# Four layers on one core: causal tiles of 64 queries shared by two heads, and the gates of a segment in one run

## The chip, the core and the metric

The kernel runs on one core of a Trainium2 chip as one program. Its time is the device time of one execution in microseconds. The engines are named as the profile names them: PE (TensorE, matrix products, with PEld for its weight loads), DVE (VectorE), ACT (ScalarE), POOL (GpSimd) and SP (SyncE, which here issues nearly all DMAs).

## The reference, cut to what matters

Two kinds of layer alternate over x of 2048 tokens x 512: an attention with a compressed memory (32 heads of 16, four segments of 512 tokens), and a gated feed-forward network with 1792 hidden columns. The weights of both attention layers are the same, and so are those of both networks.

```python
def _A_ref(x, wq, wk, wv, wo, beta):          # H = 32, Dh = 16, N = 4 segments, L = 512
    ...
    phi = lambda t: jnp.where(t > 0, t + 1.0, jnp.exp(t))
    mask = (ar[:, None] < ar[None, :]) * -1e9
    g = sigmoid(beta)
    for s in range(N):
        logits = einsum('bhqd,bhkd->bhqk', qs, ks) * scale + mask
        a_dot = einsum('bhqk,bhkd->bhqd', softmax(logits), vs)
        pq = phi(qs)
        num = einsum('bhld,bhde->bhle', pq, M)
        den = einsum('bhld,bhd->bhl', pq, z)[..., None] + 1e-06
        outs.append(g * (num / den) + (1.0 - g) * a_dot)
        pk = phi(ks)
        M = M + einsum('bhld,bhle->bhde', pk, vs)
        z = z + einsum('bhld->bhd', pk)
    return concat(outs) @ wo

def _B_ref(x, w_gate, w_up, w_down):
    return gelu(x @ w_gate) * (x @ w_up) @ w_down

x = x + _A_ref(_layernorm(x), ...)
x = x + _B_ref(_layernorm(x), ...)
x = x + _A_ref(_layernorm(x), ...)
x = x + _B_ref(_layernorm(x), ...)
```

## The kernel before

The work is cut into eight segment steps k = 0 to 7: four segments of the first pair of layers, then four of the second. x stays in SBUF (`x_sb`). Step k has an object `Att(k)` and an object `Ffn(k)`; segment k + 4 starts from the x that `Ffn(k)` left.

**Who sets the order.** The order on every engine is written out in full when the program is built. A planner (`Clocks`, `Engine`, `Item`) keeps an estimated clock for each engine; at each step of PE it picks the next thing that is ready by those clocks: a pair of score rounds (`score`), a memory product (`mem_event`), or an `Item`, a product of several matmuls that needs one of eight PSUM banks. Each item has a due time, and jobs of the other engines have slacks, all from the table `POLICY`. Where nothing is ready, PE gets a product of a constant (`warm`) as a filler. On the chip, nothing is reordered: each engine works through its list and waits by semaphores.

**Attention.** `qk` and `v` items make q, k (transposed: 4 blocks b of 128 rows, each 8 heads of 16 rows) and v. A "round" of scores is 256 columns on each of four row tiles of PE (32 rows each): it covers four of the eight heads of a block, the even ones (`par` 0, from `kf`, 16 rows) or the odd ones (`par` 1, from `kB`, a copy of k in which the even heads' rows are zero). A head has five rounds (`PIECES`), made of keys in tiles of 128 and the queries from there on: 512 + 384 + 256 + 128 = 1280 columns. So a block has 2 x 5 rounds, and `score` issues two rounds at a time (L848). One exp for 128 x 1024 empties each of the two pairs of PSUM banks into `pt` (ACT, L1285), and POOL zeroes what lies above the diagonal (L1291). After a head group's five rounds a "flush" (`flush_item`, L864) multiplies `pt` with v, on four column tiles of PE, into one bank; v carries a column that gives the softmax's sum. DVE transposes the result (L879), divides, transposes back (L894) and adds the memory's part (L897); `wo` follows.

`kB` is made by DVE (L591) for k < 4 and by four DMAs on SP per block for k of 4 and more (L588).

**Memory.** phi is exp on ACT (L648), a minimum on POOL (L666) and an addition on DVE (L652), which also sums phi k over the tokens (`zk`, by the accumulator). phi k is transposed by DMA, and the update (L769) multiplies it with v; `macc` and `zacc` hold M and z.

**Feed-forward.** The norm's rows (`Norm`, L447 to L477) are transposed by DMA, or for the steps in `BY_PE` on PE (L507 to L509). Of the 14 gate tiles of a step, 9 are copied out of PSUM by DVE or ACT (L408, L409) and get their Gelu in SBUF (L1046); the last 5 (`direct`) get it from PSUM (L972). In step 7 all 14 do (L959). DVE multiplies each up tile into the gate (L994), and `down` follows, added to x by DVE (L934).

**Dense products** go through `product`: whole (L421), or as four matmuls of 32 output rows side by side (L418), whichever avoids a change of tiling on PE.

Of the kernel before, what the change touches and what calls it, by code (L numbers as in the profile page):

```python
# [11 lines left out]
ACT = mybir.ActivationFunctionType  # L12
# [30 lines left out]
NO_DIAG = 1  # L43


def narrow(pieces, par):

    if par:
        return pieces
    return [(ki, q0 + o, min(n, 64) if n == P else n, c0 + o) for ki, q0, n, c0 in pieces  # L50
            for o in ((0, P // 2) if n == P else (0,))]
# [5 lines left out]
SETS = 3  # L57

URGENT, SOON, NORMAL = -4.0, -1.5, 0.0
XN_BUFS = 4  # L60
# [4 lines left out]
POLICY = dict(  # L65
    flush_wait=152.105, piece_slack=40.738, kb_slack=10.905, mem_slack=-2.348, margin=2.56, qk_due=0.594,
    e_q=-0.77, e_k=1.073, exp_slack=-18.49, e_slack=11.096, phi_slack=6.459, gelu_slack=-0.034, act_evict=5.372,
    first_evict=-0.382, gate_step=0.0, up_due=1.256, up_step=0.012, down_due=3.948, down_step=1.013,
    upd_due=-0.62, v0_due=1.254, x1_at=0.158, x2_at=5.744, x3_at=0.964, x3_load=17.129, cut_slack=-0.231,
    direct=5, gelu_tiles=1, phi_pool=0, kb_dve=4, rounds=2, early=0.939, starve=0.658, ahead=0.286, near=-3.652,  # L70
    cap=7, soon=1.448, am_slack=1.081, mem_wait=0.156)
# [11 lines left out]
class Engine:  # L83
# [4 lines left out]
    def __init__(self, overlap=0.0):  # L88
        self.free, self.overlap, self.jobs, self.table = 0.0, overlap, [], "exp"
        self.only, self.rival, self.port = None, None, 0.0  # L90

    def post(self, ready, slack, *steps, table=None, taken=None):

        self.jobs.append((ready, slack, steps, table, taken if taken is not None else []))

# [12 lines left out]
    def serve(self, now):  # L108

        self.jobs = [j for j in self.jobs if not j[4]]  # L110
        jobs = [j for j in self.jobs if not self.only or j[3] in (None, self.only)]
        if not jobs:
            return False
        start = max(self.free, min(j[0] for j in jobs) + self.LATENCY)
# [5 lines left out]
        self.jobs.remove(job)  # L120
        t = ready
# [18 lines left out]
class Clocks:  # L140
# [6 lines left out]
    def __init__(self):  # L147
# [7 lines left out]
        self.ev = {}  # L155

# [19 lines left out]
    def serve(self):  # L176

        again = True
        while again:
# [9 lines left out]
            first = min(self.engines, key=lambda e: max(e.free, min((j[0] for j in e.jobs), default=1e9)))  # L189
            again |= first.serve(self.pe) or any(e.serve(self.pe) for e in self.engines)  # L190
# [52 lines left out]

class Box:
# [9 lines left out]
class Policy:  # L254
    def __init__(self, values):
        self.__dict__.update(values)


def order(pol, nc, cst, seg, wrk, psp, A_x, A_wq, A_wk, A_wv, A_wo, A_beta, B_x, B_w_gate, B_w_up, B_w_down, out):
# [70 lines left out]
    bd = cst.tile([P, P], F32, name="bd")  # L330
    nc.gpsimd.memset(bd[:], 1.0)
    nc.gpsimd.affine_select(out=bd[:], in_=bd[:], pattern=[[-16, 8], [0, 16]], compare_op=ALU.is_ge,
                            fill=0.0, base=0, channel_multiplier=1)
    nc.gpsimd.affine_select(out=bd[:], in_=bd[:], pattern=[[16, 8], [0, 16]], compare_op=ALU.is_ge,
                            fill=0.0, base=15, channel_multiplier=-1)
    kBs = [cst.tile([P, KT, L], BF16, name=f"kB{i}") for i in range(SETS)]
    for kB in kBs[1:]:
        nc.vector.memset(kB[:], 0.0)
    mask2 = cst.tile([P, 2 * DH], F32, name="mask2")
    nc.vector.reduce_sum(out=mask2[:], in_=bd[:].rearrange("p (c n) -> p n c", c=4), axis=mybir.AxisListType.X)  # L340
    maskB = mask2[:, DH:DH + 1]

    tmp_e = cst.tile([P, H], F32, name="tmp_e")
    tmp_e2 = cst.tile([P, H], F32, name="tmp_e2")
    cden = cst.tile([P, H], BF16, name="cden")
    macc = cst.tile([P, 4, 2 * DH], F32, name="macc")
    e2x = cst.tile([P, 2, 2, 2, 4 * TPS], F32, name="e2x")
    zacc = cst.tile([P, 4], F32, name="zacc")
    vaugs = [cst.tile([P, TPS, VW + 15], BF16, name=f"vaug{i}")[:] for i in range(SETS)]
    vaugs.append(gel_sb[:].rearrange("p f l -> p (f l)")[:, 0:TPS * (VW + 15)].rearrange("p (t v) -> p t v", t=TPS))  # L350

    def by_head(va):
        return va[:, :, 0:VW].rearrange("p t (h e) -> p t h e", e=DH + 1)
# [1062 lines left out]
```

## Time and profile before

| | |
|---|---|
| time, median of 3 runs | 547.69 us (547.14 to 548.39) |
| the profiled execution's own time | 547.77 us |
| its span | 546.1 us |
| granted TensorE clock | 1.00 |
| PE busy | 535.6 us, 98% |
| DVE busy | 442.4 us, 81% |
| ACT busy | 445.5 us, 82% |
| POOL busy | 278.8 us, 51% |
| HBM read, written | 9.71 MB, 2.10 MB |

The busy time of an engine is a sum over stages with different limits. In the groups of instructions a row has line, engine, operation, output <- inputs, shapes and count, then the busy time in us and the mean of one in ns, then the idle time before it and what ended it. Matmuls overlap, so the mean duration of one is longer than its share of PE's time.

### The profile page before, as it was taken

The page shows a single profiled execution, that of the slowest core. Times are in us where ns is not written, and L with a number is a line of the kernel's source. Part 1 is how long each engine was busy: PE and PEld are TensorE (multiplying, and loading weights), DVE is VectorE, ACT ScalarE, POOL GpSimd, SP SyncE. Part 2 cuts the span into 40 slices and gives each one's busy share as a digit, 9 for nine tenths or more (in the row PEclk, how much of TensorE's full clock was granted, in tenths as well). Part 3 has the DMA queues.
Part 4 walks back from the last instruction along what each step waited for, and adds up shares of the span by engine and source line. Part 5 has one row for each costly group of instructions (what it writes and reads, how often), then busy time and mean ns, then how long its engine had stood idle before and what let it go on. Part 6 is the DMA issues. An engine that isn't in the chain of part 4 may idle for free.

```text
span 546.1 us, 23526 instructions
## 1 busy us (share of the span) xinstructions
PE 535.6 (98%) x10291; PEld 266.0 (49%) x10321; DVE 442.4 (81%) x880; ACT 445.5 (82%) x572; POOL 278.8 (51%) x410
## 2 busy tenths in 40 slices
PE   9999999999999999999999999999999999999997
PEld 4444444445544444444444444455454446445444
DVE  7999999779998999588987987979768796786072
ACT  5899989999999959989999899988998789910500
POOL 2687774367928847156862668724574155300000
PEclk9999999999999999999999999999999999999999
DMA  8248702500150135000224040132201003000001
GB/s 265 46 81 174 178 2 41 166 13 4 30 80 14 42 51 79 12 10 16 42 31 79 13 51 13 31 61 34 53 29 41 18 19 68 4 2 21 21 0 38
DMA packets 66983, 26.96 MB, mean 49 GB/s; under 512 B 55360, under 2 KB 66880, under 8 KB 66880
## 3 DMA queue, kind: packets, MB, share of 16 engines
q1 hardware_dynamic: 66448, 25.19, 22.9%
q8 instruction: 80, 1.31, 1.1%
q10 hardware_dynamic: 432, 0.27, 0.2%
q14 instruction: 23, 0.19, 0.1%
HBM read 9.71 MB, written 2.10 MB: 22 GB/s over the span
## 4 chain that ended last, share of the span: by engine, by line
PE 83%; DVE 12%; issue 2%; DMA 2%; ACT 0%; DVEq 0%
PE ps L418 45%; PE ps L421 21%; PE ps L848 8%; PE ps L864 6%; DVE st L447 1%; DMA phik<-e 1%; DVE byq L879 1%; PE ps L320 1%; DVE x_sb L934 1%; DVE xn L477 1%; DVE ab L887 1%; DMA xnT<-xn 1%; DVE e L652 1%; PE ps L700 1%; DVE gel_sb L408 1%
## 5 line engine op out<-in xcount | busy, mean ns | idle before, releaser
L1285 ACT ACTIVATE pt<-ps 128x1024 bf16<-128x1024 f32 x320 | 308.0, 1026 | 31.4 <-PE ps L848 22.0
L1291 POOL TENSOR_SCALAR_AFFINE_SELECT pt<-pt 128x512 bf16<-128x512 bf16 (+1 forms) x320 | 184.2, 582 | 178.0 <-ACT pt L1285 176.5
L994 DVE TENSOR_TENSOR gel_sb<-gel_sb,ps 128x512 bf16<-128x512 bf16 x112 | 75.4, 685 | 39.4 <-PE ps L421 22.2
L418 PE MATMUL ps<-wd_sb,gel_sb 128*32 128x512 bf16 (+1 forms) x1452 | 81.5, 364 | 0.0
L666 POOL TENSOR_SCALAR e<-e 128x512 bf16<-128x512 bf16 x48 | 73.8, 1541 | 5.1 <-ACT e L648 3.3
L418 PE MATMUL ps<-xnT,wg_sb 128*32 128x512 bf16 x1040 | 63.3, 380 | 0.2 <-DVE gel_sb L408 0.2
L879 DVE STREAM_TRANSPOSE byq<-ps 128x512 f32<-128x512 f32 x64 | 45.4, 709 | 17.4 <-PE ps L864 15.0
L934 DVE TENSOR_TENSOR x_sb<-x_sb,ps 128x512 bf16<-128x512 bf16 (+1 forms) x68 | 43.0, 643 | 16.5 <-PE ps L421 13.4
L418 PE MATMUL ps<-xnT,wu_sb 128*32 128x512 bf16 x956 | 55.3, 380 | 0.0
L418 PEld LDWEIGHTS <-gel_sb 128*32 128x32 bf16 x1452 | 35.9, 96 | 31.3 <-issue 6.5
L421 PE MATMUL ps<-xnT,wu_sb 128*128 128x512 bf16 x202 | 45.9, 379 | 0.7 <-issue 0.3
L421 PE MATMUL ps<-xnT,wg_sb 128*128 128x512 bf16 x178 | 40.9, 379 | 1.0 <-issue 0.5
L864 PE MATMUL ps<-pt,vaug 128*32 128x256 bf16 (+2 forms) x1568 | 40.9, 243 | 0.0
L447 DVE BATCH_NORM_STATS2 st<-x_sb 128x6 f32<-128x512 bf16 x60 | 40.5, 675 | 0.4
L418 PEld LDWEIGHTS <-wg_sb 128*32 128x32 bf16 x1040 | 26.1, 96 | 24.7 <-issue 4.2
L864 PEld LDWEIGHTS <-vaug 128*32 128x32 bf16 x1568 | 32.2, 97 | 10.0 <-issue 1.6
L418 PEld LDWEIGHTS <-wu_sb 128*32 128x32 bf16 x956 | 24.3, 97 | 25.1 <-issue 2.6
L1046 ACT ACTIVATE gel_sb<-gel_sb 128x512 bf16<-128x512 bf16 x63 | 35.0, 632 | 0.0
L418 PE MATMUL ps<-wo_sb,aT 128*32 128x512 bf16 x500 | 31.3, 380 | 0.2 <-DVE x_sb L934 0.2
L421 PEld LDWEIGHTS <-wu_sb 128*128 128x128 bf16 x209 | 19.9, 98 | 23.6 <-issue 0.2
L477 DVE TENSOR_SCALAR xn<-x_sb,mv,rs 128x512 bf16<-128x512 bf16 x64 | 30.2, 526 | 1.2 <-POOL rs L465 0.9
L848 PE MATMUL ps<-q,kf 16*128 16x256 bf16 (+1 forms) x896 | 31.0, 232 | 0.1
(128 smaller groups left out, 718.5 us busy)
## 6 DMA issues: line engine op xcount, KB each, us to landing
wg_sb<-in_B_w_gate_dram SPq DMA_DIRECT2D x8, 224.0 KB, 4.2
wu_sb<-in_B_w_up_dram SPq DMA_DIRECT2D x8, 224.0 KB, 4.1
wd_sb<-in_B_w_down_dram SPq DMA_DIRECT2D x7, 256.0 KB, 4.3
x_sb<-in_A_x_dram SPq DMA_DIRECT2D x3, 512.0 KB, 7.9
out_dram<-x_sb SPq DMA_DIRECT2D x12, 128.0 KB, 1.7
kB<-kf SPq DMA_DIRECT2D x64, 16.0 KB, 1.8
xnT<-xn SPq DMA_TRANSPOSE x48, 2.5
wv_sb<-in_A_wv_dram SPq DMA_DIRECT2D x1, 512.0 KB, 6.9
```

The costliest lines, as they stand in the source:

```text
L418: nc.tensor.matmul(out[r], lhsT=lhsT[:, r], rhs=rhs, start=start, stop=stop, tile_position=(0, 32 * c))
L421: nc.tensor.matmul(out, lhsT=lhsT, rhs=rhs, start=start, stop=stop)
L447: nc.vector.bn_stats(out=self.st6[:, 0, :], in_=x_sb[:, self.tt0 + j, :])
L477: nc.vector.tensor_scalar(out=xn[:], in0=x_sb[:, self.tt0 + j, :], scalar1=self.mv[:, j, 0:1], scalar2=self.rs[:, j, :], op0=ALU.subtract, ...
L666: return lambda: eng.tensor_scalar(out=e[0][:], in0=e[0][:], scalar1=1.0, scalar2=None, op0=ALU.min)
L848: nc.tensor.matmul(ps_all[:, pair[unit // 2], o:o + n], lhsT=lhsT[rows, b, P * ki:P * ki + P], rhs=self.q[rows, b, q0:q0 + n], start=True, ...
L864: nc.tensor.matmul(ps()[32 * j:32 * j + 32, q0:q0 + n], lhsT=self.vaug[:, ki, h * (DH + 1):h * (DH + 1) + 32], rhs=pt_all[:, slot, unit, c ...
L879: nc.vector.transpose(out=self.byq[:, par, :, :].rearrange("p a c -> p (a c)"), in_=ps()[:])
L934: ck.dve.post(ck.made(), slack, (0.15 + 0.00104 * (c1 - c0), lambda: nc.vector.tensor_tensor(out=xt, in0=xt, in1=ps()[:, 0:c1 - c0], op=AL ...
L994: ck.dve.post(ck.made(), NORMAL, (0.683, lambda: nc.vector.tensor_tensor(out=g, in0=g, in1=ps()[:], op=ALU.mult), lambda t: (ps.read(t), e ...
L1285: nc.scalar.activation(out=pt_all[:, s0, :, :].rearrange("p (h u) c -> p h (u c)", h=2), in_=ps_all[:, p0[0]:p0[1] + 1, :], func=ACT.Exp, ...
L1291: nc.gpsimd.affine_select(out=half, in_=half, pattern=[[0, w], [1, P]], compare_op=ALU.is_ge, fill=0.0, base=0, channel_multiplier=-1)
```

## The change

- **Tiles of 64 queries.** The scores of a head off the diagonal are cut at 64 queries instead of 128, and fill four rounds (`PIECES`). What is left, 64 queries against their own 64 keys at the start of each key tile, goes into one round which both heads of a pair share (`SHARED`, round `MAIN`): a 128-key product whose first 64 rows are the even head's and whose last 64 the odd head's keys. Its keys are `kX`: 64 columns in which the odd heads' rows are zero, and 128 in which the even heads' are. A block now has 9 rounds.
- `kX` is made by DVE for k = 0, and by eight DMAs on SP per block for every other k. There is one `kX` per block, so a copy waits for the scores of the step before on that block.
- The flush takes four rounds with v and the shared one with `vS`, v rearranged so that rows 0 to 63 hold the even and 64 to 127 the odd head's; two DMAs per step make it, and a flush waits for them. A flush has 40 matmuls instead of 24 or 32.
- The masks work on 64 columns, and on the shared round on 64 partitions by 256 columns, twice.
- **Gates in one run.** `direct` is 14: when the first gate of a step has been issued, the other 13 follow, no scores are issued meanwhile, and every Gelu reads PSUM.
- **The sum of phi k** comes from the update: v's extra column makes it a product of 34 columns; `zk` and `zacc` go, and one mask (`mask34`) serves M and z.
- **Start.** The constants of gate and v move from DVE to POOL, ahead of the first norm's rows; the norm of step 1 is transposed on PE; fillers are 128 columns wide instead of 512, and 32 instead of 256 ahead of a transposed tile.
- **New order.** `POLICY` has other values throughout, among them `x3_load` (the last quarter of x loads at 31.6 instead of 17.1 us of the planner's clock) and `kb_dve`.

```diff
-ROUNDS = 5
-STEPS = 8 * ROUNDS
-PIECES = [[(0, 0, 256, 0)], [(0, 256, 256, 0)], [(1, 128, 256, 0)], [(3, 384, 128, 0), (1, 384, 128, 128)],
-          [(2, 256, 256, 0)]]
+Q = P // 2
+MAIN = 4
+ROUNDS = 2 * MAIN + 1
+STEPS = KT * ROUNDS
+PIECES = [[(0, 64, 256, 0)], [(0, 320, 192, 64), (3, 448, 64, 0)], [(1, 192, 256, 0)],
+          [(2, 320, 192, 0), (1, 448, 64, 192)]]
+SHARED = [(ki, P * ki, Q, Q * ki) for ki in range(KT)]
...
-    first_evict=-0.382, gate_step=0.0, up_due=1.256, up_step=0.012, down_due=3.948, down_step=1.013,
-    upd_due=-0.62, v0_due=1.254, x1_at=0.158, x2_at=5.744, x3_at=0.964, x3_load=17.129, cut_slack=-0.231,
-    direct=5, gelu_tiles=1, phi_pool=0, kb_dve=4, rounds=2, early=0.939, starve=0.658, ahead=0.286, near=-3.652,
+POLICY = {..., 'gate_step': 0.764, 'up_due': 0.735, 'up_step': -0.024, 'down_due': 3.352, 'x3_load': 31.598, 'direct': 14, 'kb_dve': 1, 'early': 2.22, 'starve': 1.318, 'burst_slack': -4.609, 'hold': 0.287, 'late': 0.8, 'turn1': 4, 'vs_slack': 3.116}
...
+                def odd():
+                    nc.vector.tensor_scalar(out=kX[:, :, Q:], in0=keys(), scalar1=maskB, scalar2=None, op0=ALU.mult)
...
+                def copy(j, par):
+                    r = slice(32 * j + DH * par, 32 * j + DH * (par + 1))
+                    return lambda: nc.sync.dma_start(out=kX[r, :, Q:] if par else kX[r, :, 0:Q],
+                                                     in_=keys()[r] if par else keys()[r, :, 0:Q])
...
+                    for n in range(8):
+                        ck.sp.post(t, slack, (0.62, copy(n % 4, n // 4), sent if n == 7 else None))
...
-                    for j in range(4) if k >= pol.kb_dve else ():
-                        r = slice(32 * j + DH, 32 * j + 2 * DH)
-                        ck.sp.post(t, pol.kb_slack if k else URGENT, (0.62, lambda r=r: nc.sync.dma_start(
-                            out=self.kB[r, b, :], in_=self.kf[r, b, :]), kb_sent if j == 3 else None))
...
+                    ck.when(lambda: k == 0 or ("sc", k - 1, b) in ev, lambda: masked(max(t, ck.pe) if k else t))
...
+                ck.sp.post(t, pol.vs_slack, (0.62, copy(0), None), (0.62, copy(1), landed))
...
-                                                   accum_out=self.zk[:, b:b + 1] if which == "k" else None)
+                    nc.vector.scalar_tensor_tensor(out=dst, in0=src, scalar=0.0, in1=e[0][:], op0=ALU.max, op1=ALU.add)
...
-                                     rhs=by_head(self.vaug)[:, j, 8 * b + 2 * g:8 * b + 2 * g + 2, 0:DH], start=(c == 0),
+                                     rhs=by_head(self.vaug)[:, j, :, 4 * b + g, :], start=(c == 0),
...
+            for ki, q0, n, c0 in SHARED if par is None else PIECES[i % (MAIN + 1)]:
                 for j in range(4):
...
+                work = [(r + (MAIN + 1) * par, self.vaug, piece) for r in range(MAIN) for piece in PIECES[r]]
+                work += [(MAIN, self.vS, piece) for piece in SHARED]
+                for n_mm, (i, values, (ki, q0, n, c0)) in enumerate(work):
+                    for j in range(4):
...
-                              and ck.has(*[("v", k, j) for j in range(TPS)])
+                              and ck.has(("vS", k))
...
+                    if pol.direct >= FT:
+                        if self.n_gate == 1:
+                            ck.burst = FT
+                            for it in items:
+                                if it.kind == "gate" and it.after == ("xnTf", k):
+                                    it.due = -0.8
+                        ck.burst -= 1
+                        ck.act.post(ck.made(), pol.burst_slack, (0.602, lambda: nc.scalar.activation(
+                            out=gel_sb[:, ft, :], in_=ps()[:], func=ACT.Gelu_apprx_tanh),
+                            lambda t: (ps.read(t), ev.update({("gel", k, ft): t}))), table="gelu")
+                        return
...
-        if not streams or not rounds_ready(2):
+        if not streams or not rounds_ready(2) or ck.burst > pol.hold:
             return 0
...
-                nc.gpsimd.affine_select(out=half, in_=half, pattern=[[0, w], [1, P]], compare_op=ALU.is_ge, fill=0.0,
-                                        base=0, channel_multiplier=-1)
+                half = pt_all[:, slot, at[0]:4:2 if len(at) == 2 else 1, 0:Q]
+                nc.gpsimd.affine_select(out=half, in_=half, pattern=[[0, len(at)], [1, Q]], compare_op=ALU.is_ge, fill=0.0,
+                                        base=Q, channel_multiplier=-1)
+
+            def mask_shared(slot, at, par):
+                part = pt_all[Q * par:Q * (par + 1), slot, at[0]:4:2 if len(at) == 2 else 1, :]
...
-                product(ps(), warm[:], wide)
-                ck.on_pe(Clocks.MM[512])
+                product(ps()[:, 0:P], warm[:], warm[:])
+                ck.on_pe(Clocks.MM[128])
```

More of the change, by code (lines that the diff above doesn't have):

```diff
@@ L1161, in next_e @@
     def next_e():
[L1162 removed]
+        if not e_slots.free or e_slots.queue or ck.burst:
             return
@@ L1201, in rounds_now @@
         wait = backlog()
-        if pol.rounds > 2 and n >= 3 and left != 4 and wait < pol.ahead and rounds_ready(3):
-            return 3
-        if n >= 2 and left != 3 and (idle or left in (2, 4) or wait < (pol.early if streams[0][0] < 1 else pol.starve)):
+        if n >= 2 and (idle or left == 2 or wait < (pol.early if streams[0][0] < 1 else pol.starve)):
             return 2
```

333 lines of the change are left out of this document (192 added, 141 removed).

## The prediction

> **What bounds the kernel now.** I read the page first: the span, the busy times, the busy tenths and the chain that ended last.
>
> ```profile
> span 546.1 us, 23526 instructions
> PE 535.6 (98%) x10291; PEld 266.0 (49%) x10321; DVE 442.4 (81%) x880; ACT 445.5 (82%) x572; POOL 278.8 (51%) x410
> PE   9999999999999999999999999999999999999997
> PE 83%; DVE 12%; issue 2%; DMA 2%; ACT 0%; DVEq 0%
> ```
>
> PE is full in every slice but the last, and holds 83% of the chain; it sits idle for 546.1 - 535.6 = 10.5 us in all. ACT and DVE have some 100 us to spare, although not everywhere: the busy time by stretch (columns: PE, PEld, DVE, ACT, POOL) shows DVE almost without a gap while the first segment's scores run.
>
> ```profile
> 14.00:28.00 14.00, 14.00 (x275) 6.53 (x273) 13.62 (x37) 12.21 (x17) 8.41 (x14) 1.00 0.22 42
> 42.00:56.00 14.00, 13.20 (x305) 6.83 (x302) 13.86 (x29) 13.68 (x17) 10.33 (x16) 1.00 0.91 194
> ```
>
> A busy PE can still waste time, so the next view is PE's timeline (start, duration, line, shape, count). In a pipelined row the next row's start tells more than the duration.
>
> ```profile
> 209.93 1.69 PE L418 MATMUL ps<-xnT,wg_sb 128*32 128x512 bf16 x28
> 211.55 0.40 PE L848 MATMUL ps<-q,kf 16*128 16x256 bf16 x8
> 211.88 1.91 PE L418 MATMUL ps<-xnT,wg_sb 128*32 128x512 bf16 x32
> 213.72 0.41 PE L848 MATMUL ps<-q,kf 16*128 16x256 bf16 x20
> 214.06 0.40 PE L418 MATMUL ps<-xnT,wg_sb 128*32 128x512 bf16 x4
> 214.28 0.72 PE L864 MATMUL ps<-pt,vaug 128*32 128x256 bf16 x24
> 214.83 1.47 PE L418 MATMUL ps<-xnT,wg_sb 128*32 128x512 bf16 x24
> ...
> 220.08 0.73 PE L864 MATMUL ps<-pt,vaug 128*32 128x256 bf16 x32
> 220.63 2.76 PE L418 MATMUL ps<-xnT,wg_sb 128*32 128x512 bf16 x48
> ...
> 506.47 12.25 PE L421 MATMUL ps<-xnT,wg_sb 128*128 128x512 bf16 x55
> 518.56 12.25 PE L421 MATMUL ps<-xnT,wu_sb 128*128 128x512 bf16 x54
> ```
>
> The 14 gate tiles of the last segment are 56 products (one record is missing), and take 518.56 - 506.47 = 12.09 us: 0.216 us for 512 columns. Four products of 32 output rows side by side cost the same: the 28 of 209.93 are seven groups and end at 209.93 + 7 x 0.216 = 211.44. The scores start only at 211.55 and the next dense product at 211.88. So one pair of score rounds, 512 columns on four row tiles, holds PE for 211.88 - 211.44 = 0.44 us, of which 0.216 is columns and the rest two changes of tiling. The block with 20 products, 16 of them 64 columns wide, takes 214.06 - (211.88 + 8 x 0.216) = 0.45 us.
>
> **The change, part by part.** Counts of the changed kernel are those of the order in which it issues its instructions.
>
> *Fewer score rounds.* Ten rounds for each four pairs of heads become nine: both heads' diagonal tiles share one. Two rounds are issued at a time, so 4 x 8 x 10 / 2 = 160 blocks become 144: 16 x 0.44 = **-7.0 us** of PE, on the path. The same 16 blocks carry 32 exps; they and the copies below are ACT's gain.
>
> *Narrow pieces.* The scores grow from 1,792 to 2,048 products and phi V from 1,792 to 2,560, at no more columns; 64 columns is now common. Above, a block with 16 narrow products costs 0.01 us more, and the two flushes (24 products, 8 of them 128 wide, and 32, 16 of them 64 wide) both take 0.55 us. After the change every score block has narrow pieces instead of 32 of 160: (144 - 32) x 0.01 = 1.1 us; a flush has 40 products, 28 of them under 256 columns and 24 of 64, for which I take 0.01 us on 64 flushes, 0.6. Sum **+1.7**. Lower end 0, as the flush rows say. Upper end by products of 32 columns:
>
> ```profile
> 61.91 0.66 PE L769 MATMUL ps<-gel_sb,phik 128*32 128x32 bf16 x64
> 62.39 0.84 PE L418 MATMUL ps<-wo_sb,aT 128*32 128x512 bf16 x12
> ```
>
> Sixteen groups of four take 0.48 us, 0.030 each, where 32 columns alone would be 0.0135: 0.0165 on top. The (256 + 768) / 4 = 256 added groups would at that toll cost 4.2 us. I stay near the lower end, because the flush rows have the very shape.
>
> The Trainium skill, TensorEngine Tiling (Array Packing), section Instruction Overhead, speaks against this part: a matmul on trn2 carries about 60 cycles, and one of width 1 lasts as long as one of 60. Read as a floor it spares 64 columns. Read as an addition, 60 cycles are 0.025 us at 512 columns in 0.216 us, and 256 groups would cost an estimated 6.4 us instead of 1.7. The trace bears out the floor, not the addition: sixteen narrow products added nothing to a flush.
>
> *Fillers.* Where the planner found nothing for PE it issued products of a constant, and two ahead of each transposed tile:
>
> ```profile
> L418 PE MATMUL ps<-warm 128*32 128x512 bf16 x76 | 5.0, 381 | 0.0
> L507 PE MATMUL ps<-warm 128*128 128x256 bf16 x24 | 4.8, 275 | 0.8 <-DVE q L408 0.8
> L421 PE MATMUL ps<-warm 128*128 128x512 bf16 x9 | 2.3, 380 | 0.0
> ```
>
> ```profile
> 498.62 0.39 PE L507 MATMUL ps<-warm 128*128 128x256 bf16 x2
> 498.85 0.39 PE L509 MATMUL ps<-ident,xn 128*128 128x128 bf16 x4
> 499.07 0.38 PE L507 MATMUL ps<-warm 128*128 128x256 bf16 x2
> ```
>
> Now 76 / 4 + 9 = 28 of 0.216 us and 12 pairs of 0.23: 6.0 + 2.8 = 8.8 us. Then there are 120 / 4 + 48 = 78 of 128 columns, 78 x 0.054 = 4.2, and 32 of 32 columns, between 0.014 and 0.054 each: 1.0. That is **-3.6**; the other end is 0, if PE waits where it filled. Four more tiles of the second segment's norm are turned on PE, at 499.07 - 498.85 = 0.22 us: **+0.9**.
>
> *Beside the path.* These rows give the load of the others (busy, mean ns):
>
> ```profile
> L1285 ACT ACTIVATE pt<-ps 128x1024 bf16<-128x1024 f32 x320 | 308.0, 1026 | 31.4 <-PE ps L848 22.0 <-POOL pt L1291 5.1 <-PE ps L418 1.1
> L409 ACT ACTIVATE gel_sb<-ps 128x512 bf16<-128x512 f32 x32 | 18.9, 603 | 3.2 <-PE ps L418 1.6 <-PE ps L421 0.9
> L408 DVE CAST gel_sb<-ps 128x512 bf16<-128x512 f32 x35 | 23.2, 681 | 4.6 <-PE ps L418 4.5
> L972 ACT ACTIVATE gel_sb<-ps 128x512 bf16<-128x512 f32 x35 | 19.6, 594 | 0.3 <-PE ps L418 0.2
> L1285 ACT ACT_TABLE_LOAD x6 | 7.7, 1283 | 0.1
> L1291 POOL TENSOR_SCALAR_AFFINE_SELECT pt<-pt 128x512 bf16<-128x512 bf16 x192 | 128.6, 676 | 88.7 <-ACT pt L1285 88.2
> L1291 POOL TENSOR_SCALAR_AFFINE_SELECT pt<-pt 128x256 bf16<-128x256 bf16 x128 | 55.9, 440 | 89.3 <-ACT pt L1285 88.3 <-DVE rdm L718 0.5
> ```
>
> ACT loses 32 x 308.0 / 320 = 30.8 us of exps and, on balance, 13 copies of 0.6 (30 gate copies go, 17 others come from DVE): 7.9; the Gelus stay 112; two more table loads add 2.6. About -36. DVE loses 33 gate copies and those 13 others that moved, at 0.68: some -31, and the small sums of phi k. POOL's masks go from 184.5 us to 224 x 0.440 + 64 x some 0.32 + 128 x 0.676 = 206: +21, 55% of the span. None of these is on the path, so I cost them at nothing; the cover is PE's queue of dense products. If PE had waited for ACT or DVE, this part would be the gain instead.
>
> *Gates in one run.* During 14 gates (12.1 us) no scores are issued. PE has the gates; ACT needs 14 x 0.594 + 2 x 1.283 = 10.9 us and keeps up. What is late next is the first flush after the run. Last Gelu, table load, two exps and a mask take 0.59 + 1.28 + 2 x 0.96 + 0.68 = 4.5 us, and the order puts 4.3 to 5 us of ups between: I allow **+0.5** for seven runs.
>
> *New waits.* The shared round waits for masked keys, which SP copies in eight pieces for each of 28 key blocks where it made four for 16; a flush waits for the rearranged V (two copies a segment). Behind such a copy on SP stand the transposes of norms, phi k and memory output, and behind those PE. A key copy may start once the previous segment's scores on that block are done, three blocks ahead, so I cost the waits at nothing and keep their price for a rival. The last quarter of x (512 KB) now loads beside the weights instead of ahead of them: at the 194 GB/s of 42 to 56 us that delays the weights by 2.6 us.
>
> ```profile
> 64.00:68.00 4.00, 4.00 (x100) 2.13 (x99) 3.96 (x10) 4.00 (x5) 3.24 (x5) 1.00 0.01 4
> 79.72 2.33 PE L421 MATMUL ps<-xnT,wg_sb 128*128 128x512 bf16 x10
> ```
>
> DMA (the share before last) has fallen silent by 64 us and the first gates come at 79.72, so this costs nothing while the 15 us between are not used up.
>
> Sum: -7.0 + 1.7 - 3.6 + 0.9 + 0.5 = -7.5. The profiled execution took 547.77 us, 1.7 outside its span, and the median is 547.69, the same within 0.1. Forecast: 547.7 - 7.5 = **540.2 us**. With every term at its worse end (fillers 0, narrow 4.2) it is 546.3; with narrow at 0, 538.5.
>
> **The rivals.**
> *Narrow toll*: 4.2 us by the 32-column rows in place of 1.7 gives 542.7. Against it stand the equal flushes. The addition of the Trainium skill's tiling page, with its estimate of 6.4 us, would give 544.9.
> *More than the sum*: with ACT and DVE lighter, about half of PE's 10.5 us of idle time goes too (the rest is start and end): 540.2 - 5 = 535. For it: DVE at 13.86 of 14 us early on.
> *No gain*: what PE sheds comes back as waits, since the early stage is DVE's as well: 547.7. Against: DVE sheds more than PE.
> *Slower, by SP's queue.* Key copies on SP:
>
> ```profile
> 241.32 12.70 SPq L588 DMA_DIRECT2D kB<-kf  x16
> kB<-kf SPq DMA_DIRECT2D x64, 16.0 KB, 1.8
> ```
>
> Each holds SP for 12.70 / 16 = 0.79 us, a group of eight for 6.3. The norms ahead of the gates of five segments go over the same queue. If each stands behind such a group with half covered, PE waits 5 x 3.2 = 16 us: 556. It decides from 7.5 / 5 = 1.5 us of uncovered wait for each. Against it: the copies have a deadline most of a segment away, and in the order transposes stand between the groups. The Trainium skill, DMA: Bandwidth & Descriptors, Specifications, wants pieces of 512 B for line rate; these rows shrink from 1 KB to 128 and 256 B, and no row here shows such a copy.
>
> **How the numbers follow.** Forecast 0.62, narrow toll 0.12, more 0.06, no gain 0.06, slower 0.14. About 0.2%, 1.1 us, is what a measurement here can tell from no change. The first three are faster: 0.80; same 0.06; slower 0.14. The range from 534.5 to 548 holds all but the slower case and a tail below.
>
> **What would show it.** In the profile after: 144 blocks of scores, each still 0.44 to 0.45 us from dense to dense; flushes at 0.55 to 0.57; PE at 98% of a span near 538.5; ACT near 410, DVE near 410 and POOL near 300 us busy. The whole order is a new one, and a wait that I don't foresee would show as idle time. The forecast is wrong if PE's idle time grows well past 10.5 us, above all before keys, rearranged V or transposed tiles that came by DMA, or if flushes reach 0.62 us.

## The result: 1.2% slower, and where the time stands in the profile after

The changed kernel takes 553.69 us (median of 4 runs, 553.26 to 555.57), beside 547.45 us for the kernel before on the same chip. The ratio is 1.0118 [1.009, 1.0145]. The forecast was 540.2 us. Two single executions, one of the kernel before at 889 us and one of e5_thin at 1050 us, stand far above all others of their kernel and are left out throughout. The profiled execution took 553.32 us. Its page, the same lines as shown of before:

```profile
span 551.6 us, 26774 instructions
PE 530.7 (96%) x11751; PEld 281.9 (51%) x11773; DVE 403.1 (73%) x773; ACT 414.9 (75%) x529; POOL 309.4 (56%) x530
PE   7999598999999999999999999999999999999997
PEclk9999799999999999999999999999999999999999
PE 81%; DVE 10%; issue 2%; POOL 2%; DMA 1%; ACT 1%; SPq 1%; DVEq 0%; POOLq 0%; ACTq 0%
```

PE is busy for 4.9 us less than before although the span is 5.5 us longer, so its idle time has doubled from 10.5 to 20.9 us. Both lines of tenths show one place above all: the fifth slice, where PE has a 5 and the granted clock a 7. The busy time in stretches of 20 us says the same (columns: us, PE, PEld, DVE, ACT, POOL, granted clock, DMA share, GB/s). First the kernel before, then the changed one:

```profile
40.00:60.00 20.00, 19.20 (x434) 9.93 (x433) 19.83 (x40) 19.40 (x24) 14.88 (x22) 1.00 1.01 193
60.00:80.00 20.00, 19.08 (x436) 9.89 (x437) 19.13 (x40) 18.46 (x24) 16.34 (x22) 1.00 0.17 50
80.00:100.00 20.00, 19.79 (x219) 9.32 (x220) 17.94 (x40) 18.93 (x31) 6.86 (x7) 1.00 0.28 48
```

```profile
40.00:60.00 20.00, 19.16 (x624) 11.13 (x616) 16.03 (x30) 19.35 (x24) 15.72 (x33) 1.00 0.60 131
60.00:80.00 20.00, 14.87 (x355) 8.74 (x348) 13.99 (x27) 12.13 (x14) 12.08 (x20) 0.83 0.61 136
80.00:100.00 20.00, 17.85 (x289) 9.38 (x284) 11.66 (x28) 15.06 (x25) 6.74 (x9) 1.00 0.39 90
```

From 60 to 80 us every engine is emptier than before: DVE has 6 us to spare, ACT 8, POOL 8. So no engine's work is the bound there. Three timelines around that place (start, duration, what, count, and in brackets the idle time before it with what ended it) give the chain. PE of the changed kernel:

```profile
57.81 1.09 PE L462 MATMUL ps<-warm 128*32 128x128 bf16 x64
59.74 0.35 PE L462 MATMUL ps<-warm 128*32 128x128 bf16 x12 [0.84 <-issue]
65.22 0.62 PE L915 MATMUL ps<-q,kf 16*128 16x256 bf16 x12 [5.13 <-DVE byq L946]
65.77 2.53 PE L465 MATMUL ps<-warm 128*128 128x128 bf16 x22
```

PE issues fillers and then stops for 5.13 us until DVE has transposed a flush (`byq`, L946), because that frees a PSUM bank. When it runs again the 22 products of 128 columns take 2.3 us to the next row at 68.09, 0.105 each, where 128 columns at full speed take 0.054. DVE:

```profile
51.98 1.40 DVE L521 TENSOR_SCALAR xn<-x_sb,mv,rs 128x512 bf16<-128x512 bf16 x3
64.13 0.41 DVE L521 TENSOR_SCALAR xn<-x_sb,mv,rs 128x512 bf16<-128x512 bf16 x1 [6.92 <-DMA xnT<-xn]
```

DVE wrote three normalised rows of step 3's norm by 53.4, and later, at 57.2, stood for 6.92 us before the fourth. There are three buffers for these rows now (`XN_BUFS`, four before; the list under The change leaves this out), and the fourth row may be written only when the first has been transposed by DMA. The flush that PE needs stood behind this row in DVE's list. And SP, first the changed kernel, then the one before:

```profile
49.87 1.32 SPq L676 DMA_DIRECT2D vS<-vaug  x2
52.69 6.75 SPq L640 DMA_DIRECT2D kX<-kf  x8
60.17 2.23 SPq L428 DMA_TRANSPOSE xnT<-xn  x1
63.12 2.50 SPq L428 DMA_TRANSPOSE xnT<-xn  x2
67.31 1.20 SPq L428 DMA_TRANSPOSE xnT<-xn  x1
```

```profile
44.85 5.70 SPq L384 DMA_TRANSPOSE xnT<-xn  x4
```

The rows that were ready by 53.4 are transposed from 60.17 on: eight key copies of step 1 (6.75 us) stand ahead of them. Before, the same four transposes were issued between 44.85 and 50.55, with no key copy near them. Adding up SP's issuing durations by stretch, SP was held 2% of the time between 60 and 80 us before, and 90% after; over the span 206 us and 329 us.

The clock record in steps of 1 us has the granted clock at 0.50 from 62.0 to 68.9, 6.8 us; PE worked in the last 3.7 us of it, which costs some 1.8 us.

**The account.** For each pair of successive products in both traces I took the time from start to start, less the columns at 0.42 ns each (0.216 us for 512) and 0.1 us for a change of tiling; what is left over 0.03 us counts as waiting, gaps of a missing record left out. Before: 9.5 us of 546.1. After: 23.3 of 551.6. So PE's own work fell from 536.6 to 528.3, by 8.3 us, and waits rose by 13.8. Of these, 8.0 are the stop at 59 us (1.0 + 5.2, and some 1.8 by the clock), 1.1 the start (below), and 1.5 and 1.2 two waits in flushes; some 2 are small. The count depends on how a missing record is told from a wait, and is good to 1 or 2 us. The two flushes:

```profile
86.08 0.52 PE L932 MATMUL ps<-pt,vaug 128*32 128x192 bf16 x20 [1.47 <-issue]
209.22 0.25 PE L932 MATMUL ps<-pt,vS 128*32 128x64 bf16 x9 [1.07 <-issue]
```

These two, and the 0.84 us before 59.74, stand as `issue`: in the middle of a flush or of fillers, PE waits for nothing that the view names. The list of DMA queues on the page has a queue that carries instructions (packets, MB, share), before and then after:

```profile
q8 instruction: 80, 1.31, 1.1%
q8 instruction: 92, 1.51, 1.1%
```

Both come to some 64 bytes for each instruction of PE and PEld (1.31 MB for 20,612 and 1.51 MB for 23,524), so this queue seems to feed PE, 16 KB at a time. In the traces of the changed kernel and of all its variants there are 31 such stops over 0.25 us, and each ends 1.2 to 1.7 us after a packet of q8 has come in; the kernel before and e4_before_xn3 have no such stop. So PE probably ran out of instructions there, of which narrow pieces and fillers need more for the same columns. No run varied this, so it is argued and not shown. By it, 3.7 of the 13.8 us, 1.0 of the stop at 59 us among them, would not come from SP's list.

### The profile page after: what moved, and what is told of

It reads as the page before. It is cut to its first block, busy times and chain, and to the rows that moved or that the text cites. A ratio compares the mean times of both kernels' runs of the same rounds, so it can differ in the third digit from the quotient of the medians.

```text
span 551.6 us, 26774 instructions
## 1 busy us (share of the span) xinstructions
PE 530.7 (96%) x11751; PEld 281.9 (51%) x11773; DVE 403.1 (73%) x773; ACT 414.9 (75%) x529; POOL 309.4 (56%) x530
## 3 DMA queue, kind: packets, MB, share of 16 engines
q8 instruction: 92, 1.51, 1.1%
## 4 chain that ended last, share of the span: by engine, by line
PE 81%; DVE 10%; issue 2%; POOL 2%; DMA 1%; ACT 1%; SPq 1%; DVEq 0%; POOLq 0%; ACTq 0%
PE ps L462 48%; PE ps L465 18%; PE ps L915 7%; PE ps L932 6%; DVE x_sb L1002 2%; DVE st L491 1%; DVE xn L521 1%; DVE byq L946 1%; DMA xnT<-xn 1%; DVE gel_sb L1074 1%; PE ps L780 1%; PE ps L849 1%; SPq L428 1%; POOL pt L1376 1%; POOL pt L1382 1%
## 5 line engine op out<-in xcount | busy, mean ns | idle before, releaser
L1372 ACT ACTIVATE pt<-ps 128x1024 bf16<-128x1024 f32 x288 | 275.6, 1031 | 49.2 <-PE ps L915 45.7
L1376 POOL TENSOR_SCALAR_AFFINE_SELECT pt<-pt 128x256 bf16<-128x256 bf16 (+1 forms) x288 | 120.2, 428 | 157.5 <-ACT pt L1372 152.6
L1382 POOL TENSOR_SCALAR_AFFINE_SELECT pt<-pt 64x512 bf16<-64x512 bf16 x128 | 90.4, 707 | 4.2
L462 PE MATMUL ps<-xnT,wu_sb 128*32 128x512 bf16 x1272 | 77.0, 380 | 0.6 <-DVE gel_sb L1074 0.6
L1039 ACT ACTIVATE gel_sb<-ps 128x512 bf16<-128x512 f32 x98 | 56.5, 600 | 20.2 <-PE ps L462 11.4
L946 DVE STREAM_TRANSPOSE byq<-ps 128x512 f32<-128x512 f32 x64 | 45.3, 708 | 9.8 <-PE ps L932 9.3
L521 DVE TENSOR_SCALAR xn<-x_sb,mv,rs 128x512 bf16<-128x512 bf16 x63 | 28.4, 489 | 25.5 <-DMA xnT<-xn 21.7
L462 PEld LDWEIGHTS <-wu_sb 128*32 128x32 bf16 x1272 | 31.1, 96 | 30.9 <-issue 2.3
L932 PE MATMUL ps<-pt,vaug 128*32 128x256 bf16 (+2 forms) x1344 | 34.9, 238 | 1.9 <-issue 1.5
L915 PEld LDWEIGHTS <-kX 32*128 32x128 bf16 x1280 | 19.6, 93 | 31.8 <-issue 30.1
L462 PE MATMUL ps<-xnT,wq_sb 128*32 128x512 bf16 x464 | 32.2, 381 | 0.0
L915 PE MATMUL ps<-q,kX 32*128 32x64 bf16 (+2 forms) x1120 | 32.0, 218 | 0.1
```

The lines of the kernel that those rows point to most:

```text
L462: nc.tensor.matmul(out[r], lhsT=lhsT[:, r], rhs=rhs, start=start, stop=stop, tile_position=(0, 32 * c))
L915: nc.tensor.matmul(ps_all[:, pair[unit // 2], o:o + n], lhsT=lhsT, rhs=self.q[rows, b, q0:q0 + n], start=True, stop=True, tile_position=(3 ...
L932: nc.tensor.matmul(ps()[32 * j:32 * j + 32, q0:q0 + n], lhsT=values[:, c:c + 32], rhs=pt_all[:, slot, unit, c0:c0 + n], start=n_mm == 0, s ...
L946: nc.vector.transpose(out=self.byq[:, par, :, :].rearrange("p a c -> p (a c)"), in_=ps()[:])
L1039: ck.act.post(ck.made(), pol.burst_slack, (0.602, lambda: nc.scalar.activation(out=gel_sb[:, ft, :], in_=ps()[:], func=ACT.Gelu_apprx_tanh ...
L1372: nc.scalar.activation(out=dst, in_=src, func=ACT.Exp, scale=SCALE)
```

## The experiments

The theory at the outset: SP's queue with its 224 key copies makes the transposes late. The rivals: the number of buffers alone; the order at one place alone; the bytes of the small pieces on the DMA engines. The orders of all engines are those of the changed kernel (in e4_before_xn3 of the kernel before) except where the edit says otherwise. Medians are over each kernel's runs; ratios are to the kernel before on the same chip (548.17, 548.01 and 547.82 us on the three chips).

**A buffer of its own for the fourth row (e1_row).**

```diff
-            xn = seg.tile([P, D], BF16, tag=f"xn{i}", ...)[:] if i < XN_BUFS else spare_room(D)
+            own = self.key == ("xnTa", 3) and j == TPS - 1
+            xn = (spare_room(D) if own or i >= XN_BUFS else seg.tile([P, D], BF16, tag=f"xn{i}", ...)[:])
```

> The changed kernel, with one buffer more for one row: the fourth normed row of step 3 is written to space of its own instead of the first of three buffers, so DVE need not wait there for a transpose. Orders of all engines as in the changed kernel. Queue theory (eight key copies on SP ahead of the transposes, and three buffers where there were four, stop DVE for 6.9 us at 57 us; PE starves for about 6 us and then runs 6.8 us at half clock): the wait of 6.9 us goes, the clock stays at 1.00, and the time falls by 6 + 3.4, to about 544 us. Spread theory (the loss is many small waits for keys, rearranged V and gate runs in all segments): under 1 us of gain, 553 us, and the clock drop moves elsewhere.

Measured: 555.16 us (553.57 to 556.54), 1.0129 [1.0103, 1.0154]. A miss. DVE no longer stops at 57 us, but PE stops some 7 us later than in the changed kernel (from 66.95 instead of 60.09), for the same transposes. PE's and SP's timelines of this run:

```profile
73.50 0.62 PE L462 MATMUL ps<-xnT,wq_sb 128*32 128x512 bf16 x4 [6.55 <-DMA xnT<-gel_sb]
```

```profile
67.30 1.20 SPq L428 DMA_TRANSPOSE xnT<-gel_sb  x1
```

The fourth transpose is issued at 67.30, where it was at 67.31: SP sets its time, not the buffer. The wait has only moved from DVE to PE. The time lies nearer the 553 of the spread theory, but not for its reason: it is still one long stop.

**Half of the key copies left out (e2_half).** The even heads' copies are not made, so the shared round works on incomplete keys; SP has four copies a block in place of eight.

```diff
-   return lambda: nc.sync.dma_start(out=kX[r, :, Q:] if par else kX[r, :, 0:Q], in_=...)
+   return lambda: par and nc.sync.dma_start(out=kX[r, :, Q:], in_=keys()[r])
```

> The changed kernel without the even half of the key copies (four DMAs per block instead of eight; the shared round then works with incomplete keys). Orders otherwise as in the changed kernel. Queue theory: SP gets through the first 60 us about 5 us earlier, the stop of DVE shrinks from 6.9 us to under 2 and PE does not starve: 543 to 546 us. Spread theory: each segment gains something, 548 to 551, with the stop at 57 us still there. If DMA bandwidth of the late load of x and of the weights were the cause, nothing changes: these copies are 8 KB each.

Measured: 546.08 us (544.74 to 547.03), 0.996 [0.9944, 0.9975]: 7.6 us below the changed kernel, as the queue theory had it. DVE's and SP's timelines:

```profile
57.34 0.72 DVE L521 TENSOR_SCALAR xn<-x_sb,mv,rs 128x512 bf16<-128x512 bf16 x1
```

```profile
60.59 1.20 SPq L428 DMA_TRANSPOSE xnT<-xn  x1
```

With the same three buffers the fourth row no longer waits; the last transpose is issued 6.7 us earlier, and the granted clock is 1.00 throughout. PE's longest stop is 1.5 us. These four copies a block carried bytes as well as issues, so the run alone doesn't tell the two apart.

**One group of copies moved back (e3_order).** The eight copies of step 1's block 1 are issued behind the third transpose of step 3's norm.

```diff
+                        if (k, b) == (1, 1):
+                            send = lambda send=send: held.append(send)
...
+            while held and len(behind) == after:    # after = 3 for ("xnTa", 3)
+                held.pop(0)()
```

> The changed kernel with one group moved on SP: the eight key copies of step 1, block 1, stand behind the third transpose of step 3's norm instead of ahead of the first. Three buffers and all other orders as in the changed kernel. Queue theory: the transposes start about 6 us earlier, DVE's wait falls from 6.9 to about 1 us, the clock stays at 1.00: 544 us, as with the extra buffer. Bandwidth theory (the weights and the late load of x hold the transposes up): no change, 553 us. If the moved keys come too late for the scores of block 1, a wait of some us appears before those instead.

Measured: 553.54 us (552.79 to 554.49), 1.0101 [1.0085, 1.0117]. A miss. The first three transposes go out from 53.26 to 57.9 now, but the fourth stands behind the moved group (SP's timeline), and PE waits for it (PE's timeline), with the granted clock at 0.50 for 3.4 us from 70.3 on:

```profile
65.68 1.24 SPq L431 DMA_TRANSPOSE xnT<-xn  x1
```

```profile
70.16 0.52 PE L471 MATMUL ps<-xnT,wq_sb 128*32 128x512 bf16 x4 [2.97 <-DMA xnT<-xn]
```

So it isn't the one group ahead of the one row: the queue holds more than it can issue in this stretch, and whoever is put back is late.

**The kernel before with three buffers (e4_before_xn3).**

```diff
-            xn = seg.tile([P, D], BF16, tag=f"xn{i}", bufs=1, name="xn")
+            xn = seg.tile([P, D], BF16, tag=f"xn{turn[0] % 3}" if turn[0] > 3 else f"xn{i}", bufs=1, name="xn")
+            turn[0] += 1
```

> The kernel before, with three buffers for normed rows in place of four, in rotation, and every engine's order unchanged. Queue theory: three buffers alone cost little where SP isn't crowded, a transpose being 1.2 us apart: 547 to 549 us. If three buffers alone were the cause, DVE stops in several norms here too and the time rises by 5 us or more, to 552.

Measured: 577.30 us (576.76 to 577.42), 1.0534 [1.0517, 1.0552]. A large miss. The waits of this run, grouped (us in total, times, longest), and its granted clock:

```profile
DVE xn L479 <- DMA xnT<-xn: 25.5, 11, 3.9
PEclk9998999999999999999999999989999999999999
```

An order written for four buffers pays for the fourth in 11 places. The run doesn't price the buffers in the changed kernel, whose order was written for three and where DVE waits 21.7 us in four such places, only one of which (6.92) stops PE for more than 0.6 us. It shows that a buffer removed under an unchanged order is not free, which I had thought it to be.

**The same copies with a sixteenth of the bytes (e5_thin).** Each copy moves one row of 16, so the keys of the shared rounds are incomplete.

```diff
-                    r = slice(32 * j + DH * par, 32 * j + DH * (par + 1))
+                    r = slice(32 * j + DH * par, 32 * j + DH * par + 1)
```

> The changed kernel with all its key copies on SP, but each of one row instead of 16 (15 of 16 rows are not copied, so the shared and the odd rounds work with incomplete keys): as many issues on SP, a sixteenth of the bytes and packets. Issue theory (SP's time per DMA, 0.6 to 0.7 us each, is what delays everything behind it): the stop in the first 70 us stays and the time is 552 to 555 us. Transfer theory (the small packets of the copies fill the DMA engines or the queue behind them): as with half of the copies left out, 544 to 547 us.

Measured: 550.19 us (547.53 to 552.74), 1.0042 [1.0021, 1.0062], between the two expectations. The runs spread over 5 us and the profile was taken in the fastest (547.53; last transpose of step 3's norm at 61.15), so it doesn't stand for the median. That run alone has a granted clock of 1.000 on record; the other eight have 0.997 to 0.991, those of the changed kernel 0.994 to 0.991. In the profile a copy holds SP for 0.58 us on the average, where the changed kernel's holds it for 0.70. Inconclusive: the number of issues and what is moved both seem to have a share, the second in part by a longer hold of SP.

**Even heads' keys by DVE (e6_even).** One DVE instruction a block, which the kernel has for step 0 (`even`), in place of four copies.

```diff
+                def make(j, par):
+                    return by_dve(j, par) if (False if par else True) else copy(j, par)
...
-                        ck.sp.post(t, slack, (0.62, copy(n % 4, n // 4), sent if n == 7 else None))
+                        ck.sp.post(t, slack, (0.62, make(n % 4, n // 4), sent if n == 7 else None))
```

> The changed kernel with the even half of the key copies replaced by one DVE instruction per block (the one that step 0 uses), at the place where the first of the four copies was issued; the orders are otherwise those of the changed kernel. Issue theory: as with that half left out, less 28 x 0.26 us of DVE that may or may not be covered: 546 to 548 us. If DVE is too full for it, 550 or more.

Measured: 545.69 us (545.4 to 547.52), 0.996 [0.9946, 0.9974]. The whole computation is done, with 112 copies off SP and 28 instructions more on DVE, and 8 us are back. The profiled run is the slowest of the five (547.52): in it DVE still waits 3.39 us for a transpose before the fourth row, and the granted clock is 0.50 for 3.4 us; the four others have 1.000 on record.

**The same, with step 1's odd keys by DVE and an earlier start (e7_even_s).** The zeroing of rearranged V's buffers moves ahead of the reduction for which DVE waits at the start.

```diff
+                    return by_dve(j, par) if (k == 1 if par else True) else copy(j, par)
...
+    for vs, eng in zip(vSs, (nc.vector, nc.gpsimd, nc.vector)):     # ahead of the masks' reduction
+        eng.memset(vs, 0.0)
```

> As the run before, and step 1's odd keys made by DVE too, and DVE's two memsets at the start issued ahead of the reduction that waits for POOL. Issue theory: SP falls behind less before 70 us, and the first scores come 1.1 us earlier: 543 to 545 us, faster than both kernels. Otherwise 546 or more.

Measured: 544.65 us (543.67 to 545.26), 0.9937 [0.9922, 0.9951]: faster than both kernels. Its page and SP's timeline:

```profile
span 543.5 us, 26528 instructions
PE 532.6 (98%) x11773; PEld 280.7 (52%) x11773; DVE 410.5 (76%) x805; ACT 414.3 (76%) x529; POOL 309.8 (57%) x530
```

```profile
59.59 1.20 SPq L428 DMA_TRANSPOSE xnT<-xn  x1
```

**All keys by DVE (e8_all_s).** As e7_even_s, with `make` always giving DVE's instruction.

> All keys of the shared and odd rounds made by DVE, at the places where the copies were issued, and the memsets moved as in the run before: SP issues 224 DMAs fewer. Issue theory: 540 to 543 us, near the sum of the work that was forecast. If 28 x 0.6 = 17 us more of DVE work collides with its deadlines, 545 to 550.

Measured: 546.23 us (545.96 to 547.21), 0.997 [0.9958, 0.9982], the fallback. The stop is gone and the clock is 1.00, but PE's waits are 17.4 us by the account above, against 15.8 in e7_even_s. The likely reason, not followed wait by wait, is that DVE's added instructions come at places where PE soon needs DVE; by the times, what is left on SP of steps 2 to 7 does no more harm there than on DVE.

**The start alone (e9_start).** Only the memsets of e7_even_s.

> The changed kernel with one thing moved: the zeroing of the three buffers of rearranged V stands ahead of the reduction that makes the masks, so that DVE does not do it between that reduction and the first statistics. Everything else and every order is the same. If the lost 1.1 us of the start is carried to the end: 552.5 us (553.69 - 1.14), ratio to the changed kernel 0.998. If SP's queue sets the pace of the first 70 us, the earlier start is taken back there: 553.3 to 554, and PE stops before step 3's transposes as long as before, about 5 us, with the half clock after it.

Measured: 553.15 us (548.75 to 555.47), 1.0091 [1.0058, 1.0124]: no difference from the changed kernel that these runs can tell. First scores come at 10.27 in place of 11.58, but SP's timeline and PE's show it taken back:

```profile
71.37 6.52 SPq L640 DMA_DIRECT2D kX<-kf  x8
77.98 1.25 SPq L428 DMA_TRANSPOSE phik<-e  x1
```

```profile
62.42 0.40 PE L915 MATMUL ps<-q,kf 16*128 16x256 bf16 x12 [2.48 <-DVE byq L946]
81.88 0.57 PE L849 MATMUL ps<-gel_sb,phik 128*32 128x34 bf16 x52 [2.69 <-DMA phik<-e]
```

PE stops 2.65 us less for the same flush, the granted clock is at 0.50 for 3.4 us instead of 6.8, and then PE waits 2.69 us for a transpose of phi k behind eight more copies.

**Step 1's copies from POOL's queue, and from ACT's (e10_pool, e11_act).** The same 32 copies, the same bytes and pieces.

```diff
-   return lambda: nc.sync.dma_start(out=kX[r, :, Q:] if par else kX[r, :, 0:Q], ...)
+   return lambda: (nc.gpsimd if k == 1 else nc.sync).dma_start(...)       # e11_act: nc.scalar
```

> The changed kernel with the 32 key copies of step 1 issued from POOL's queue in place of SP's: the same copies, bytes and pieces, in the same order. Theory 'issue' (SP is held 0.6 to 0.7 us by each copy, and the transposes stand behind them): SP is rid of 32 x 0.7 = 22 us before 100 us, the stop of DVE and PE at 58 us and the half clock go, 545 to 549 us. Theory 'transfer' (the small pieces keep the DMA engines, whoever issues them): the transposes land as late as before, 552 to 555 us, with the half clock. A third way: POOL, held by its issues, hands masks out late, and PE waits before flushes: 550 or more without the half clock at 58 us.

> The same with ACT's queue in place of POOL's. Theory 'issue': the stop at 58 us and the half clock go; ACT pays 32 x 0.6 = 19 us in its first 100 us, where it is busy 3 of 4 us, so that some of it shows in late exps: 546 to 552 us. Theory 'transfer': 552 to 555 us with the stop where it was. If both this run and the one by POOL lose the stop, it was SP's issuing, not the bytes.

Measured: 557.26 us (556.9 to 558.76), 1.0175 [1.0157, 1.0194], and 559.10 us (556.44 to 560.48), 1.0202 [1.0175, 1.0229]. By POOL it went the third way, and further than its price. SP's timeline, the group of POOL's copies (busy, mean ns), and PE's timeline of that run:

```profile
54.24 2.03 SPq L428 DMA_TRANSPOSE xnT<-xn  x1
62.16 2.56 SPq L428 DMA_TRANSPOSE xnT<-xn  x1
```

```profile
L640 POOL DMA_DIRECT2D kX<-kf x32 | 17.0, 533 | 0.0
```

```profile
58.40 0.29 PE L932 MATMUL ps<-pt,gel_sb 128*32 128x192 bf16 x8 [1.10 <-POOL pt L1376]
59.73 0.30 PE L932 MATMUL ps<-pt,gel_sb 128*32 128x64 bf16 x14 [1.04 <-POOL pt L1382]
```

The first transpose goes out within a microsecond of its row (53.71 and 54.24) although the same bytes move in the same stretch, so what held it in the changed kernel was its place in SP's list. But POOL, held 17 us, now gives out masks late, and PE waits before flushes. By ACT the first transpose is on time too (57.34, its row written from 56.90 on) and DVE doesn't stop, but PE waits for exps, 2.30 us at 74.79 and 2.29 at 78.38, with the clock at 0.50 between 76 and 80. So both runs lose DVE's stop although the bytes are the same: the transfers alone, issued elsewhere, don't bring it about. POOL, 56% busy on the average, and ACT, 75%, had no room for these issues in the first 100 us.

## Why the prediction was wrong, point by point

**Fewer score blocks, narrow pieces: right.** PE's timeline after, in the first segment:

```profile
45.83 0.73 PE L932 MATMUL ps<-pt,gel_sb 128*32 128x256 bf16 x40
46.38 1.04 PE L462 MATMUL ps<-xnT,wq_sb 128*32 128x512 bf16 x16
47.35 0.40 PE L915 MATMUL ps<-wd_sb 16*128 16x192 bf16 x12
47.68 1.05 PE L462 MATMUL ps<-xnT,wk_sb 128*32 128x512 bf16 x16
```

A flush of 40 products takes 0.55 us from start to start, as those of 24 and 32 did. A score block holds PE from the end of the 16 dense products (46.38 + 4 x 0.216 = 47.24) to 47.68, 0.44 us. The addition that the Trainium skill's TensorEngine Tiling (Array Packing), Instruction Overhead, could be read to state is not there; the floor is what the trace bears out. The whole of PE's work fell by 8.3 us in this profile, and by 7.9 to 9.1 in those of e1_row to e8_all_s with the same products (span less waits 527.5 to 528.7), where the terms for blocks, pieces, fillers and turned tiles gave 8.0. So the sum of PE's work was right within what this count can tell, although its single terms, the 0.5 us for the gate runs among them, can't be told apart here. What narrow pieces may cost besides is the wait for instructions above, for which the prediction has no term.

**The load of the others: near.** ACT 414.9, DVE 403.1 and POOL 309.4 us, where 410, 410 and 300 were forecast.

**New waits at nothing: the step that failed.** It said that a key copy may start three blocks ahead, and, against the rival, that its deadline is most of a segment away; so it cost the waits at nothing. Nothing in the profiles speaks against that for the copy itself. It doesn't hold for what stands behind it: the transposes of step 3's norm, whose first row was ready at 53 us and which PE needed, through DVE, at 60. The step named these transposes and then priced the copy's own deadline. In its place the profile shows 6.75 us of copies on SP, 6.92 us of DVE and 5.13 us of PE waiting behind them, and 6.8 us of half clock. Nor had the prediction a term for the third of three buffers; with a fourth for this row, PE stops at the transpose itself (e1_row). The price of the step, for half of the copies alone, is the difference between the changed kernel and e6_even: 553.69 - 545.69 = 8.0 us by the medians, and (1.0118 - 0.996) x 547.5 = 8.7 by the ratios to the kernel before.

**The late quarter of x "costs nothing": open.** The step looked at the weights. The DMA share of the changed kernel is 0.61 from 60 to 80 us, not near nothing, but the first gates, at 87.79, follow without a wait. What moved is the norm: the quarter of x is issued at 39.32 us, and the norm's rows are written from 51.98, where they were written at 43.96 before: 8 us of slack were gone before SP's queue took its part. That quarter loaded early in the new order wasn't tried, so its own share stays open.

**The start: left out.** DVE zeroes rearranged V between the reduction and the first statistics. After, then before (DVE's timeline, and the first scores on PE's):

```profile
2.41 0.38 DVE L365 TENSOR_REDUCE mask<-gel_sb 128x32 f32<-128x128 f32 x1 [1.36 <-POOL gel_sb L361]
2.96 0.97 DVE L386 MEMSET vS<- 128x1096 uint32 x1 [0.18 <-issue]
5.00 1.23 DVE L1149 BATCH_NORM_STATS2 st<-x_sb 128x6 f32<-128x512 bf16 x2
```

```profile
11.58 0.37 PE L915 MATMUL ps<-wd_sb 16*128 16x256 bf16 x8
```

```profile
10.44 0.40 PE L848 MATMUL ps<-wd_sb 16*128 16x256 bf16 x8
```

1.14 us at the scores. By itself it is worth little in the changed kernel (e9_start); beside a queue that isn't full it may count, but e7_even_s changed two things and doesn't separate them.

**The rival "slower, by SP's queue": the right mechanism in another place.** It expected five norms ahead of the gates to pay 3.2 us each and came to 556. One norm paid visibly, in the first 70 us, and its price came by way of DVE's list, a PSUM bank and the clock. That its 556 lies near the 553.69 measured is luck. The condition it gave, 1.5 us of uncovered wait for each, could have been looked for in the order that was at hand: three buffers, eight copies ahead of the first transpose, and a flush behind the fourth row on DVE. Its chance of 0.14 was too low for that.

**What stays open.** e7_even_s is still 4.4 us over the forecast. Its waits are 15.8 us against 9.5 before; the longest is a stop of 1.64 us that ends at 59.55 and that all versions of the changed order have in some form (0.84 to 2.47), with a half clock behind it, and the rest are of 1 us and less. The stop is one of those that end soon after a load of instructions; no run tried wider fillers or fewer narrow pieces against it, and the causes of the rest were not followed one by one. Nor is it settled how SP's load splits between the number of issues and the time that the small pieces take (e5_thin).

## What to carry to other kernels

A DMA's price is not its own deadline but that of whatever stands behind it on the queue that issues it: list, for each queue, the next thing behind each new group of issues and who needs it when. Follow a late transfer through in-order engines to PE; giving the first one that stops another buffer moves the wait and doesn't end it. When many small copies overfill a queue, one instruction on an engine with slack can replace four of them, but only while that engine is not needed at once (half of the copies on DVE gained 8 us; all of them gained no more). And where PE stops in the middle of many short products and the profile names no cause, set the stop beside the loads of instructions.

## What the runs showed of the hardware that was not expected

The small copies cost more than their bytes. The page's part on DMA issues after (count, KB each, median us from issue to landing):

```profile
kX<-kf SPq DMA_DIRECT2D x112, 8.0 KB, 2.6
kX<-kf SPq DMA_DIRECT2D x112, 16.0 KB, 1.9
```

The copy of 8 KB, in pieces half as long, lands later than that of 16 KB. It also comes first in each group of eight, and where the 16 KB copies go alone (e2_half) they take 2.2 us, so how much of the difference is due to the pieces stays open. A copy holds SP for 0.70 us on the average, and still for 0.58 with a sixteenth of the bytes (e5_thin). The Trainium skill, DMA: Bandwidth & Descriptors, section Issuing engines are not separate DMA queues, says that spreading DMAs over engines saves only the sequencer's time to initiate them, "usually small relative to the DMA itself". Here that time is a quarter to over a third of the time to landing, and it was the queue that ran full.

The granted clock halves when PE runs dry: 2 us after the long stop began in the changed kernel (60.1 to 62.0), 5 us in e1_row (66.9 to 71.9), and both times for 6.8 us. The Trainium skill, TensorE: Matmul & The Clock Gate, Part 1, tells of a free-running activity window of about 3.4 us; 6.8 us is twice that, and the differing delays agree with a window that doesn't start with the stop. The clock records of this case bear it out further. Of the stretches at 0.50, all that don't run into the end of the program last 3.41 or 6.83 us. Where one trace has several, they start whole multiples of 3.413 us apart, whatever PE did in between: 27.31 and 324.27 us in e4_before_xn3 (8 and 95 times), 27.31 in e11_act.

So a stop of 5 to 6.5 us cost 1.8 to 2.6 us more than it lasted. A short one can bring it too: in e7_even_s, PE lost only 1.64 us between 56 and 60, and the granted clock was 0.57 from 60 to 64, while a stop of 1.65 us at the same place in e8_all_s left it at 1.00. Part of the spread between runs of one kernel is this: a stretch of 3.41 us at 0.50 takes 0.003 off the mean clock, and the four runs of the changed kernel have 0.994, 0.991, 0.994 and 0.993.
